# The second layer of a fused attention and MoE kernel: its first two products by Strassen's seven block products, its last product as a separate stage

## The chip, the cores and the metric

The kernel is one program on one core of a Trainium2 chip. The metric is the time on the device in microseconds (us), the median of several executions; lower is better. Engines: PE is TensorE (matmuls), PEld its weight loads, DVE VectorE, ACT ScalarE, POOL GpSimd, SP SyncE, which here issues the DMAs (SPq is its queue).

## What is computed

```python
# q, k, v: (4, 8, 576, 64), s: (4, 8, 576)
attn_out = _attn_ref(q, k, v, s)                  # causal attention, bias from a running sum of max(s, 0)
x = attn_out.transpose(0, 2, 1, 3).reshape(2304, 512)
# first layer: w_in (512, 2048), w_out (2048, 512)
h = x @ w_in;  r = maximum(h, 0);  x = (s * r * r + b) @ w_out
# second layer: w_a, w_b (512, 1536), w_out (1536, 512)
a = x @ w_a;   b = x @ w_b;        out = (a * b) @ w_out
```

The weights of both layers arrive as float64.

## The kernel before

Every matmul of the layers runs on operands that are split in a high and a low float32r part, three matmuls for one product (high by high, high by low, low by high). A matmul takes 128 rows of contraction, 128 output rows and up to 512 columns.

The order of the whole program is written by the kernel itself. Each piece of work is an op with an engine, a cost and a due time (`Plan.op`, line 65); `Plan.order` (line 111) goes through them like a list scheduler, always giving an engine the ready op with the lowest due time, and `Plan.emit` (line 206) writes the instructions in the order found. Buffers belong to a `Tag` with so many slots. A tag with `in_order` hands its slots out in the order in which the buffers were declared, whatever the due times are. An op with `room` starts only when all the buffers named there can be had at once. On the chip each engine then runs its own list strictly in that order and waits on semaphores; SP runs all DMA issues in one list.

Tokens come in nine chunks of 256 (`NCK`). Attention and the first layer take the first part of the program. `last_two` (line 884) ends the first layer for chunks 7 and 8 together: per slice f of the hidden features `h_slice` and `y_slice`. It writes y, the first layer's output, to DRAM (`y_dr`, stored transposed: 128 features by tokens) through four evictions in the two slots of `t_r`. As `last_two` goes on, the 16 slots of `t_w` (8 KB each) that hold the first layer's weights come free, one per slice.

The second layer goes over five chunks of tokens (four of 512, one of 256) and, in each, over `NF2` = 12 slices of 128 features. `y_load` (line 983) loads a chunk of y and splits it (ACT line 992, DVE line 994). `ab_unit` (line 1026) makes 12 matmuls for a and 12 for b (line 1035), copies a out of PSUM on ACT (line 1043), multiplies on DVE (line 1044) and splits the product (lines 1047, 1048). `o_unit` (line 1053) follows `LAG` = 2 units behind and adds the slice's part of the output, 3 matmuls for each tile of 128 tokens (line 1063), into four PSUM banks, which are evicted at the chunk's end (line 1072). All weights of the second layer, 18 pieces of 1 MB, stay in SBUF; `split_w` (line 425) loads a piece as float64 words, turns it to float32 with integer operations (ACT lines 441 and 444, DVE lines 448, 450, 453) and splits it (ACT line 456, DVE line 457). The two calls of `barrier` kind that matter here are `third`, at the end of attention, and `fourth` (line 958), at the end of the first layer, which reopens its SBUF and PSUM for the second.

PSUM banks: `t_h` 2, `t_y` 2, `t_s` 4 (line 298), the last replaced by `t_o` behind `fourth`.

Of the kernel before, what the change touches and what calls it, by code (L numbers as in the profile page):

```python
# [224 lines left out]
def fused_kernel(  # L225
# [732 lines left out]
    def fourth():  # L958
        moe_ctx.close()
        psat_ctx.close()  # L960
        open_pool("ph2b", ctx)
        pools["ps_o"] = ctx.enter_context(
            tc.tile_pool(name="ps_o", bufs=1, space=PSUM, side="right", reuse_waits="tile")
        )

    moe_tags = {t_x, t_xl, t_g, t_r, t_s}
    ready3 = [op("X", 0.0, 0.0, fourth, after=[o for o in plan.ops if any(b.tag in moe_tags for b in o.bufs)])]

    t_wx = tag("ph2", [P, 2, 2, DM], F32R, 3 * NF2 // 2 - NF1, "wx")
    t_wraw = tag("ph2", [P, 2, DM, 2], U32, 2, "wraw")  # L970
    t_yraw = tag("ph2", [P, 512], F32, 2, "yraw")
    t_yh = [tag("ph2", [P, 2, 512], F32R, KC, "yhl"), tag("ph2b", [P, 2, 512], F32R, KC, "yhl")]
    t_a = tag("ph2b", [P, 512], F32, 2, "a")
    t_ab = tag("ph2b", [P, 512], F32, 2, "ab")
    t_abh = tag("ph2b", [P, 2, 512], F32R, 3, "abh")
    t_ob = tag("ph2b", [P, DM], F32, 2, "ob")
    t_o = [tag("ps_o", [P, 512], F32, 1, f"o{i}") for i in range(4)]

    chunks = [(t, min(2 * N, NT - t)) for t in range(0, NT, 2 * N)]
    y_t = {}  # L980
    BASE = 500.0

    def y_load(i, pr):
        n = chunks[i][1]
        for c in range(KC):
            raw = Buf(t_yraw, f"yr{i}{c}")
            yt = Buf(t_yh[i % 2], f"yh{i}{c}")
            y_t[i, c] = yt
            af = ready3 if i % 2 else ready2
            op(SP, 0.35, pr, lambda raw=raw, c=c: nc.sync.dma_start(raw.t[:, :n], y_dr.t[i, c, :, :n]),  # L990
               r=[(y_dr, (ck, c // 2 if ck < NCK - 2 else c)) for ck in range(2 * i, min(2 * i + 2, NCK))], w=[raw], dma=262144, after=ready2)
            op(ACT, 0.55, pr, lambda raw=raw, yt=yt: nc.scalar.copy(yt.t[:, 0, :n], raw.t[:, :n]), r=[raw], w=[(yt, 0)],
               after=af)
            op(DVE, 0.65, pr, lambda raw=raw, yt=yt: nc.vector.tensor_tensor(
                out=yt.t[:, 1, :n], in0=raw.t[:, :n], in1=as32(yt.t[:, 0, :n]), op=ALU.subtract
            ), r=[raw, (yt, 0)], w=[(yt, 1)])

    ab_w, o_w = {}, {}
    n_w2 = [0]

    def w2_load(d, i, src):
        pos = BASE - 60.0 + 4.2 * n_w2[0]
        n_w2[0] += 1
        d[i] = Buf(t_wx if n_w2[0] <= 3 * NF2 // 2 - NF1 else t_w, f"w2_{n_w2[0]}")
        raw = Buf(t_wraw, f"raw2_{n_w2[0]}")
        n0 = len(plan.ops)
        split_w(raw, d[i], src, n_w2[0] % 2 == 1, pos, pos)
        plan.after(n0, ready2)
# [7 lines left out]
    plan.after = after
    for f in range(NF2):
        w2_load(ab_w, f, w2ab[f])
        if f % 2 == 0:
            w2_load(o_w, f // 2, w2o[f // 2])  # L1020
        if f == 0:
            y_load(0, BASE - 58.0)

    ab_t, o_t = {}, {}

    def ab_unit(i, f, pr):
        n = chunks[i][1]
        ps = [Buf(t_h, f"a{i}_{f}"), Buf(t_y, f"b{i}_{f}")]
        for d in range(2):
            def go(d=d):  # L1030
                w = ab_w[f].t[:, d].rearrange("p a (c f) -> p a c f", c=KC)
                m = 0
                for c in range(KC):
                    for wi, yi in ((0, 0), (0, 1), (1, 0)):
                        nc.tensor.matmul(  # L1035
                            ps[d].t[:, :n], w[:, wi, c, :], y_t[i, c].t[:, yi, :n], start=m == 0, stop=m == 3 * KC - 1
                        )
                        m += 1

            op(PE, 12 * (n / 2400 + 0.0135), M + pr, go, r=[ab_w[f], *(y_t[i, c] for c in range(KC))], w=[ps[d]], late=0.15, room=ps)  # L1040
        a, ab, hl = Buf(t_a, f"as{i}_{f}"), Buf(t_ab, f"ab{i}_{f}"), Buf(t_abh, f"abh{i}_{f}")
        e = pr - M
        op(ACT, 0.5, e, lambda: nc.scalar.copy(a.t[:, :n], ps[0].t[:, :n]), r=[ps[0]], w=[a], late=0.1, after=ready3)  # L1043
        op(DVE, 0.63, e, lambda: nc.vector.tensor_tensor(  # L1044
            out=ab.t[:, :n], in0=ps[1].t[:, :n], in1=a.t[:, :n], op=ALU.mult
        ), r=[ps[1], a], w=[ab], late=0.08)
        op(ACT, 0.55, e, lambda: nc.scalar.copy(hl.t[:, 0, :n], ab.t[:, :n]), r=[ab], w=[(hl, 0)], late=0.1)  # L1047
        op(DVE, 0.63, e, lambda: nc.vector.tensor_tensor(  # L1048
            out=hl.t[:, 1, :n], in0=ab.t[:, :n], in1=as32(hl.t[:, 0, :n]), op=ALU.subtract
        ), r=[ab, (hl, 0)], w=[(hl, 1)], late=0.08)  # L1050
        ab_t[i, f] = hl

    def o_unit(i, f, pr):
        t0, n = chunks[i]
        hl = ab_t.pop((i, f))
        for tt in range(n // P):
            if f == 0:
                o_t[i, tt] = Buf(t_o[tt], f"o{i}{tt}")
            ops_ = o_t[i, tt]

            def go(tt=tt, ops_=ops_):
                for wi, ai in ((0, 0), (1, 0), (0, 1)):
                    nc.tensor.matmul(  # L1063
                        ops_.t, hl.t[:, ai, tt * P : (tt + 1) * P], o_w[f // 2].t[:, f % 2, wi, :],
                        start=f == 0 and wi == 0 and ai == 0, stop=f == NF2 - 1 and ai == 1,
                    )
# [9 lines left out]
    todo = [(i, f) for i in range(len(chunks)) for f in range(NF2)]  # L1076
    for j, (i, f) in enumerate(todo):
        pr = BASE + 8.2 * j
        if f == 2 and i + 1 < len(chunks):
# [105 lines left out]
```

## Time and profile before

| | |
|---|---|
| median of 3 runs | 1045.38 us (1044.62, 1045.38, 1047.78) |
| span of the profiled execution, first to last instruction | 1049.0 us, 3.6 us above the median |
| PE busy | 1018.3 us, 97% of the span |
| PEld, DVE, ACT, POOL busy | 911.7, 572.3, 522.4, 34.7 us |
| mean granted clock of TensorE | 0.998 |
| DMA | 106.6 MB, 102 GB/s on average |

The page shows one execution. Its span is the only time of that execution on the page; the sum in the prediction is made against it and then set against the median. Busy time of an engine is the union of its instructions; a matmul's own duration (its mean in ns) is longer than the distance to the next one, since matmuls are pipelined, so the cost of a row of matmuls is read from the chain of work, where pieces are cut without overlap.

### The profile page before, as it was taken

What the parts mean: (1) busy time and instruction counts of PE and PEld (TensorE: products, weight loads), DVE (VectorE), ACT (ScalarE), POOL (GpSimd) and SP (SyncE); (2) the same over time, 40 slices, a digit from 0 to 9 for tenths busy, and PEclk for the clock granted to TensorE, in tenths of its full rate; (3) what the DMA queues carried; (4) which work ended last, traced back from release to release, by engine and by line L of the source; (5) the groups of instructions that cost most, each with busy time, mean ns of one, the idle gap of its engine ahead of it and who ended that gap; (6) DMA issues with size and microseconds to landing.
All of it is one profiled execution on the core that took longest, in us unless ns stands there. A gap on an engine that the chain in (4) does not pass through costs nothing.

```text
span 1049.0 us, 17029 instructions
## 1 busy us (share of the span) xinstructions
PE 1018.3 (97%) x6808; PEld 911.7 (87%) x6808; DVE 572.3 (55%) x1005; ACT 522.4 (50%) x1029; POOL 34.7 (3%) x63
## 2 busy tenths in 40 slices
PE   4698999999999999999999999999999999999998
PEld 4598999999999999999988888888888888888897
DVE  6889764578888878796688774122113111211121
ACT  4778984568787878785465652122112111111121
POOL 4121001100000000000000000000000000000000
PEclk9999999999999999999999999999999999999999
DMA  9958523456768676866634460011002000100010
GB/s 228 226 153 211 154 81 67 117 133 173 148 142 179 145 173 139 165 134 136 235 115 145 159 210 27 1 41 41 1 1 71 0 1 11 41 1 1 1 41 21
DMA packets 137103, 106.63 MB, mean 102 GB/s; under 512 B 113088, under 2 KB 120512, under 8 KB 132672
## 3 DMA queue, kind: packets, MB, share of 16 engines
q1 hardware_dynamic: 137024, 105.55, 40.3%
q8 instruction: 53, 0.87, 0.3%
q14 instruction: 26, 0.21, 0.1%
HBM read 68.46 MB, written 10.78 MB: 76 GB/s over the span
## 4 chain that ended last, share of the span: by engine, by line
PE 85%; DVE 5%; DMA 5%; ACT 3%; issue 1%; POOL 0%; SPq 0%; DVEq 0%; POOLq 0%; ACTq 0%
PE y L867 15%; PE h L847 15%; PE b L1035 14%; PE a L1035 14%; PE o L1063 14%; PE av L562 6%; PE s L612 3%; PE s L764 3%; DMA raw<-in_w2ab_dram 2%; DVE raw L450 1%; DVE w L457 1%; DMA raw<-in_w2o_dram 1%; DVE raw L453 1%; ACT raw L441 1%; DMA tr<-hl 1%
## 5 line engine op out<-in xcount | busy, mean ns | idle before, releaser
L1044 DVE TENSOR_TENSOR ab<-b,as 128x512 f32<-128x512 f32 (+1 forms) x60 | 38.2, 638 | 274.0 <-PE b L1035 274.0
L847 PE MATMUL h<-x_all,w 128*128 128x256 f32 x1344 | 180.1, 286 | 2.4 <-ACT r L816 2.4
L867 PE MATMUL y<-g,w 128*128 128x256 f32 x1344 | 181.6, 287 | 0.0
L847 PEld LDWEIGHTS h<-x_all,w 128*128 128x128 f32 x1344 | 168.8, 193 | 3.4 <-ACT r L816 2.6
L867 PEld LDWEIGHTS y<-g,w 128*128 128x128 f32 x1344 | 167.7, 192 | 1.5
L1035 PE MATMUL b<-yh,w 128*128 128x512 f32 (+1 forms) x720 | 157.6, 368 | 0.0
L1035 PE MATMUL a<-yh,w 128*128 128x512 f32 (+1 forms) x720 | 157.5, 368 | 0.0
L1063 PE MATMUL o<-w,abh 128*128 128x512 f32 x648 | 156.6, 389 | 0.0
L1035 PEld LDWEIGHTS a<-yh,w 128*128 128x128 f32 x720 | 127.0, 188 | 23.4
L1035 PEld LDWEIGHTS b<-yh,w 128*128 128x128 f32 x720 | 126.3, 189 | 22.5
L1063 PEld LDWEIGHTS o<-w,abh 128*128 128x128 f32 x648 | 120.9, 188 | 24.6
L1043 ACT COPY as<-a 128x512 f32<-128x512 f32 (+1 forms) x60 | 32.5, 544 | 178.8 <-PE a L1035 178.6
L1047 ACT CAST abh<-ab 128x512 fp32r<-128x512 f32 (+1 forms) x60 | 34.6, 579 | 129.9 <-DVE ab L1044 129.9
L562 PE MATMUL av<-tr,vt 128*64 128x320 f16 (+4 forms) x1120 | 65.0, 274 | 13.2 <-DMA tr<-hl 8.1
L562 PEld LDWEIGHTS <-vt 128*64 128x64 bf16 x1120 | 54.9, 116 | 24.0 <-issue 9.2
L526 ACT ACTIVATE hl<-p,rc 128x256 f16<-128x256 f32 (+3 forms) x128 | 66.1, 561 | 3.5 <-DVE rc L543 3.3
L528 DVE SCALAR_TENSOR_TENSOR hl<-p,rc,hl 128x256 f16<-128x256 f32 (+3 forms) x128 | 66.0, 548 | 1.3 <-ACT hl L526 1.2
L1048 DVE TENSOR_TENSOR abh<-ab,abh 128x512 fp32r<-128x512 f32 (+1 forms) x60 | 38.2, 637 | 32.4 <-ACT abh L1047 32.3
L612 PE MATMUL s<-kq 66*128 66x256 f32 (+1 forms) x128 | 44.3, 471 | 10.3 <-DMA kq<-sums 7.8
L450 DVE SCALAR_TENSOR_TENSOR raw<-raw 128x1024 uint32<-128x1024 uint32 x34 | 41.6, 1224 | 22.5 <-ACT raw L444 20.1
L441 ACT ACTIVATE raw<-raw 128x1024 f32<-128x1024 f32 x34 | 39.6, 1163 | 25.1 <-DMA raw<-in_w2ab_dram 17.4
L456 ACT CAST w<-raw 128x1024 fp32r<-128x1024 f32 x34 | 38.7, 1148 | 18.8 <-DVE raw L453 18.5
(305 smaller groups left out, 1192.1 us busy)
## 6 DMA issues: line engine op xcount, KB each, us to landing
raw<-in_w_dram SPq DMA_DIRECT2D x16, 1024.0 KB
raw<-in_w2ab_dram SPq DMA_DIRECT2D x12, 1024.0 KB
rk<-in_k_dram SPq DMA_DIRECT2D x16, 576.0 KB
raw<-in_w2o_dram SPq DMA_DIRECT2D x6, 1024.0 KB
rq<-in_q_dram SPq DMA_DIRECT2D x16, 352.0 KB
rv<-in_v_dram SPq DMA_DIRECT2D x16, 320.0 KB
out_dram<-ob SPq DMA_DIRECT2D x18, 256.0 KB
yr<-y_dr SPq DMA_DIRECT2D x16, 256.0 KB
```

The lines of the kernel that those rows point to most:

```text
L441: op(ACT, 1.07, pr, lambda: nc.scalar.activation(hi32(), hi32(), AF.Copy, scale=2.0**-112), w=[(raw, "hi")])
L450: op(DVE, 1.15, pr, lambda: nc.vector.scalar_tensor_tensor(out=lo(), in0=hi(), scalar=0x80000000, in1=lo(), op0=ALU.bitwise_and, op1=ALU.b ...
L456: op(ACT, 1.05, pr, lambda: nc.scalar.copy(wt.t[:, :, 0, :], hi32()), r=[(raw, "hi")], w=[(wt, 0)])
L526: nc.scalar.activation(o, i_, AF.Copy, scale=r_)
L528: nc.vector.scalar_tensor_tensor(out=o, in0=i_, scalar=r_, in1=place()[:, k0:k1, 0, :cols], op0=ALU.mult, op1=ALU.subtract)
L562: nc.tensor.matmul(ap.t[64 * h : 64 * h + 64, :w], vap(j, h, vi), t[:, j, a, h, :w], start=j == 0 and m == 0, stop=j == nkt - 1 and m == 4,)
L612: nc.tensor.matmul(o, qt[:66, x, h, ti * P : (ti + 1) * P], kt[:66, x, h, :w], start=True, stop=False)
L847: nc.tensor.matmul(o, w[:, wi, c, :], x_t[ck, c].t[:, xi], start=m == 0, stop=m == 3 * KC - 1)
L867: nc.tensor.matmul(o, w1_t[2 * fp + j].t[:, 1, wi, e * P : (e + 1) * P], g.t[:, gi, j], start=fp == 0 and e % 2 == 0 and j == wi == gi == ...
L1035: nc.tensor.matmul(ps[d].t[:, :n], w[:, wi, c, :], y_t[i, c].t[:, yi, :n], start=m == 0, stop=m == 3 * KC - 1)
L1044: op(DVE, 0.63, e, lambda: nc.vector.tensor_tensor(out=ab.t[:, :n], in0=ps[1].t[:, :n], in1=a.t[:, :n], op=ALU.mult), r=[ps[1], a], w=[ab] ...
L1063: nc.tensor.matmul(ops_.t, hl.t[:, ai, tt * P : (tt + 1) * P], o_w[f // 2].t[:, f % 2, wi, :], start=f == 0 and wi == 0 and ai == 0, stop= ...
```

## The change

The two products a = x w_a and b = x w_b are formed differently for the first 2048 tokens. The contraction of 512 features is cut in two halves, the 1536 output features in two halves (slice i goes with slice i + 6, so `NFH` = 6 pairs of slices) and 1024 tokens in two blocks of 512 (`NPR` = 2 such pairs). For each pair of slices i, each matrix m (a or b) and each pair of token blocks j, `group` makes seven products of 6 matmuls in place of eight, from sums and differences of blocks. The last 256 tokens are done as before (`conv`).

- The host lays `w2ab` out by blocks. `w2_slice` loads 1 MB, decodes it as before (`decode`, the first part of `split_w`), forms four block sums on POOL and splits both the blocks and the sums into two tiles of a ring of five.
- `x_pair(j)` loads the four y blocks of each feature tile, subtracts on DVE and keeps seven split operands in `t_w` for the whole stage; `x_conv` does the last 256 tokens. Their loads share `t_yraw`, 4 slots, handed out in the order of the calls: `x_pair(0)`, `x_conv`, `x_pair(1)`.
- A group uses one bank of `t_h` and two of `t_s`, taken together at its first product; products 4 to 7 add onto banks that were read in between. DVE adds bank and running sums, and for b multiplies with a, which waits in `at`.
- a*b goes to DRAM (`ab_dr`) in float32, and after all groups a last stage loads it, splits it, and multiplies with w_out (`ab_load`, `o_unit`), chunk by chunk.
- `fourth` goes; the PSUM and SBUF of the first layer stay and are reused tag by tag (`share`).

```diff
-    NF2 = w2ab.shape[0]
+    NF2 = 2 * w2ab.shape[0]
...
+    NFH = NF2 // 2
+    t_ring = tag("ph2", [P, 4, 2, 2 * P], F32R, 5, "ring")
+    t_wraw = tag("ph2", [P, 2, DM, 2], U32, 1, "wraw")
+    t_sum = tag("ph2", [P, 4, 2 * P], F32, 1, "wsum")
+    t_yraw = tag("ph2", [P, 512], F32, 4, "yraw")
+    t_su = Tag(lambda n: moe.tile([P, 2, 512], F32, tag="g", bufs=3, name=n), 3, False, t_g)
+    t_u = Tag(lambda n: moe.tile([P, 512], F32, tag="r", bufs=2, name=n), 2, False, t_r)
...
+    ab_dr = dram_buf([2, NFH, P, NT], F32, "ab_dr")
+    BASE = 610.0
+    NPR = NT // (4 * N)
...
+    def w2_slice(m, i, pos, n):
...
+        words = decode(raw, w2ab[i, m], n % 2 == 1, pos, pos)
...
+        for z, (q, x, y, f_) in enumerate((
+            (0, lambda: blk(3), lambda: blk(2), ALU.add), (1, lambda: sm.t[:, 0], lambda: blk(0), ALU.subtract),
+            (2, lambda: blk(0), lambda: blk(3), ALU.subtract), (3, lambda: blk(1), lambda: sm.t[:, 1], ALU.subtract),
+        )):
+            op(POOL, 0.75, pos + 0.1, lambda q=q, x=x, y=y, f_=f_: nc.gpsimd.tensor_tensor(out=sm.t[:, q], in0=x(), in1=y(), op=f_),
...
+        for t, k_, rd, src in ((wa, 0.0, (raw, "hi"), lambda: words(1).bitcast(F32).rearrange("p a (b n) -> p (a b) n", n=2 * P)),
+                               (ws, 0.2, sm, lambda: sm.t)):
+            op(ACT, 1.08, pos + k_, lambda t=t, src=src: nc.scalar.copy(t.t[:, :, 0], src()), r=[rd], w=[(t, 0)])
+            op(DVE, 1.12, pos + k_, lambda t=t, src=src: nc.vector.tensor_tensor(
+                out=t.t[:, :, 1], in0=src(), in1=as32(t.t[:, :, 0]), op=ALU.subtract
...
+    def x_pair(j, pos):
...
+        for kt in range(2):
...
+            split("11", r["11"])
+            sub(r["11"], r["12"], r["11"])
+            split("22", r["22"])
+            sub(r["12"], r["22"], r["12"])
+            sub(r["22"], r["22"], r["11"])
+            split("d1", r["11"])
+            split("21", r["21"])
+            sub(r["21"], r["21"], r["22"])
+            split("d2", r["22"])
+            split("d3", r["12"])
+            split("d4", r["21"])
...
+    def group(i, m, j, pr):
...
+        b1, b2, b3 = Buf(t_h, f"b1{nm}"), Buf(t_s, f"b2{nm}"), Buf(t_s, f"b3{nm}")
...
+        def product(z, bank, wt, q, n_, first, last):
+            x = X[j, n_]
+            op(PE, 1.37, M + pr + z, lambda: mm6(bank.t, wt, q, x, lambda kt, xi: x.t[:, kt, xi], first, last),
+               r=[wt, x], w=[bank], late=0.15, room=[b1, b2, b3] if z == 0 else ())
...
+        product(0.0, b1, wa, 0, "11", True, True)
...
+        op(ACT, 0.5, e, lambda: nc.scalar.copy(s1(), b1.t), r=[b1], w=[(su, 0)], late=0.1)
...
+        product(0.5, b2, ws, 1, "d2", True, True)
+        add(u2, (su, 1), s1, b2, [(su, 0)])
+        product(1.0, b3, ws, 0, "d1", True, True)
+        product(1.5, b1, wa, 1, "21", False, True)
+        if m == 0:
+            op(ACT, 0.5, e, lambda: nc.scalar.copy(at.t[:, 0], b1.t), r=[b1], w=[(at, 0)], late=0.1)
+        else:
+            times(0, lambda: b1.t, b1)
+        product(2.0, b2, ws, 2, "d3", False, True)
+        add(lambda: u3.t, u3, s1, b2, [(su, 0)])
...
+        add(dst(3, lambda: u3.t), key(3, u3), lambda: u3.t, b3, [u3])
...
+        product(2.5, b2, wa, 2, "d4", False, True)
+        add(dst(2, s1), key(2, (su, 0)), s1, b2, [(su, 0)])
...
+        product(3.0, b3, ws, 3, "22", False, True)
+        add(dst(1, u2), key(1, (su, 1)), u2, b3, [(su, 1)])
+        if m:
+            times(1, u2, (su, 1))
+            for fh in (0, 1):
+                op(SP, 0.4, e, lambda fh=fh: nc.sync.dma_start(
+                    ab_dr.t[fh, i, :, j * 4 * N : (j + 1) * 4 * N], at.t[:, 2 * fh : 2 * fh + 2].rearrange("p a n -> p (a n)")
...
+    PER = 60.0
+    for m in range(2):
+        w2_slice(m, 0, 440.0 + 10.0 * m, m)
+    x_pair(0, 500.0)
+    x_conv(BASE + 2.0)
+    x_pair(1, BASE + 1.0)
+    for i in range(NFH):
+        p0 = BASE + PER * i
+        for m in range(2):
+            group(i, m, 0, p0 + 8.0 * m)
+        for m in range(2):
+            conv(i, m, p0 + 16.0 + 4.0 * m)
+        for m in range(2):
+            group(i, m, 1, p0 + 24.0 + 8.0 * m)
+        if i + 1 < NFH:
+            for m in range(2):
+                w2_slice(m, i + 1, p0 + 4.0 + 20.0 * m, m)
...
+    for f in range(NFH):
+        o_w[f] = Buf(t_w, f"wo{f}")
...
+        split_w(raw, o_w[f], w2o[f], f % 2 == 1, EP - 50.0 + 5.0 * f, EP - 50.0 + 5.0 * f)
...
+    def o_unit(c, f, pr):
...
+            op(PE, 1.37, M + pr, go, r=[hl, o_w[f]], w=[bank], late=0.15)
...
+    for z, (c, f) in enumerate(units):
+        ab_load(c, f, EP - 20.0 + 6.0 * z)
+    for z, (c, f) in enumerate(units):
+        o_unit(c, f, EP + 6.0 * z)
```

## Rows read from the trace of the kernel before

**Rows 1.** The page: busy time of each engine, share of the span, instructions.

```profile
PE 1018.3 (97%) x6808; PEld 911.7 (87%) x6808; DVE 572.3 (55%) x1005; ACT 522.4 (50%) x1029; POOL 34.7 (3%) x63
```

**Rows 2.** The stretches: length, busy time of each engine, PEclk, DMA share, GB/s.

```profile
515.00:602.04 87.04, 86.42 (x380) 70.95 (x379) 68.70 (x76) 51.89 (x63) 0.00 (x0) 1.00 0.45 155
602.04:1044.85 442.81, 442.80 (x2088) 372.01 (x2087) 110.44 (x164) 92.36 (x157) 0.00 (x0) 1.00 0.09 29
```

**Rows 3.** The chain that ended last, in order: start, us, what.

```profile
602.04 2.72 PE a L1035 x12
604.76 2.72 PE b L1035 x12
...
618.36 2.72 PE o L1063 x12
...
1002.39 1.39 PE o L1063 x6
1003.78 1.43 PE a L1035 x12
1005.21 1.44 PE b L1035 x12
...
1040.73 4.12 PE o L1063 x18
...
1044.87 0.69 DVE ob L1072
```

**Rows 4.** Groups by line: busy us, mean ns of one, idle before and its releaser.

```profile
L450 DVE SCALAR_TENSOR_TENSOR raw<-raw 128x1024 uint32<-128x1024 uint32 x34 | 41.6, 1224 | 22.5 <-ACT raw L444 20.1 <-ACT raw L441 1.5
L457 DVE TENSOR_TENSOR w<-raw,w 128x1024 fp32r<-128x1024 f32 x34 | 41.3, 1221 | 7.0 <-ACT w L456 7.0
L448 DVE TENSOR_SCALAR raw<-raw 128x1024 uint32<-128x1024 uint32 x17 | 11.7, 687 | 1.6 <-DMA raw<-in_w2ab_dram 1.3 <-DMA raw<-in_w_dram 0.3
L1044 DVE TENSOR_TENSOR ab<-b,as 128x512 f32<-128x512 f32 (+1 forms) x60 | 38.2, 638 | 274.0 <-PE b L1035 274.0
L994 DVE TENSOR_TENSOR yh<-yr,yh 128x512 fp32r<-128x512 f32 (+1 forms) x20 | 12.1, 634 | 6.2 <-ACT yh L992 6.2
L352 POOL CAST vt<-rv 128x512 bf16<-128x512 f32 x16 | 11.3, 708 | 138.3 <-issue 84.9 <-DVE rv L354 31.4 <-PE av L562 20.3
```

**Rows 5.** Timeline where the layers meet: start, us, engine, line, what, idle before.

```profile
598.45 0.75 DVE L832 SCALAR_TENSOR_TENSOR gg<-rr,sb_b,gg 128x512 fp32r<-128x512 f32 x1
...
599.25 2.79 PE L912 MATMUL yy<-gg,w 128*128 128x512 f32 x11 [0.17 <-DVE gg L832]
...
602.02 1.79 SPq L924 DMA_DIRECT2D y_dr<-yyo  x4
...
605.05 0.68 DVE L921 COPY yyo<-yy 128x512 f32<-128x512 f32 x1
605.76 1.92 SPq L924 DMA_DIRECT2D y_dr<-yyo  x4
...
607.78 0.64 SPq L437 DMA_DIRECT2D raw<-in_w2ab_dram  x1
...
615.43 1.17 ACT L441 ACTIVATE raw<-raw 128x1024 f32<-128x1024 f32 x1 [2.04 <-DMA raw<-in_w2ab_dram]
```

**Rows 6.** Timeline inside the second layer: a unit and the operations that read it.

```profile
705.23 2.88 PE L1035 MATMUL b<-yh,w 128*128 128x512 f32 x12
...
708.22 0.69 DVE L1044 TENSOR_TENSOR ab<-b,as 128x512 f32<-128x512 f32 x1 [6.09 <-PE b L1035]
```

**Rows 7.** Slices of 4 us in the first layer, columns as in Rows 2.

```profile
88.00:92.00 4.00, 1.77 (x15) 1.56 (x14) 3.93 (x6) 2.85 (x6) 0.00 (x0) 1.00 1.35 168
92.00:96.00 4.00, 3.83 (x21) 3.65 (x22) 3.47 (x5) 4.00 (x12) 0.61 (x1) 0.69 0.48 195
96.00:100.00 4.00, 4.00 (x30) 3.87 (x29) 3.93 (x7) 3.37 (x7) 1.34 (x2) 0.88 0.01 3
```

**Rows 8.** Timeline of PE in the same place: the matmuls that ended a wait.

```profile
92.17 1.88 PE L847 MATMUL h<-x_all,w 128*128 128x256 f32 x12 [2.41 <-ACT r L816]
```

More of the change, by code (lines that the diff above doesn't have):

```diff
@@ L956, in fused_kernel @@
     ])]
[L958 to L1008, printed above, removed]
+    ready3 = [op("X", 0.0, 0.0, lambda: None, after=[o for o in plan.ops if any(b.tag is t_x for b in o.bufs)])]
@@ L1014, in after @@
                 o.wait += 1
[L1016 to L1041, printed above, removed]
-        e = pr - M
[L1043 to L1051, printed above, removed]
@@ new lines, in split2, with y_rows @@
+    def split2(rd, hi, lo, src, pr):
+        op(ACT, 0.55, pr, lambda: nc.scalar.copy(hi(), src()), r=[rd], w=[(lo[0], (lo[1], 0))])
+        op(DVE, 0.65, pr, lambda: nc.vector.tensor_tensor(out=lo[2](), in0=src(), in1=as32(hi()), op=ALU.subtract),
+           r=[rd, (lo[0], (lo[1], 0))], w=[(lo[0], (lo[1], 1))])
+    X = {}
+    NAMES = ("11", "22", "d1", "21", "d2", "d3", "d4")
+    def y_rows(u, e):
+        return [(y_dr, (ck, e // 2 if ck < NCK - 2 else e)) for ck in (2 * u, 2 * u + 1) if ck < NCK]
@@ new lines, in x_conv, with half @@
+    def x_conv(pos):
+        X["c"] = Buf(t_w, "xc")
+        n0 = len(plan.ops)
+        u = NCK // 2
+        def half(e, hl):
+            v_ = X["c"].t.rearrange("p a b n -> p (a b n)").rearrange("p (k h n) -> p k h n", k=KC, h=2)
+            return v_[:, e : e + 2, hl]
+        for e in (0, 2):
+            raw = Buf(t_yraw, f"yrc{e}")
+            src = lambda raw=raw: raw.t.rearrange("p (e n) -> p e n", e=2)
+            op(SP, 0.35, pos, lambda src=src, e=e: nc.sync.dma_start(src(), y_dr.t[u, e : e + 2, :, :N].rearrange("e p n -> p e n")),
+               r=[(y_dr, (2 * u, e + z)) for z in range(2)], w=[raw], dma=262144)
+            split2(raw, lambda e=e: half(e, 0), (X["c"], e, lambda e=e: half(e, 1)), src, pos)
+        after(n0, ready2)
@@ new lines, in fused_kernel, with conv, go @@
+    ac_t = {}
+    def conv(i, m, pr):
+        wa, _ = ring[m, i]
+        x = X["c"]
+        bank = Buf(t_y, f"bc{i}{m}")
+        e = pr - M
+        for fh in range(2):
+            def go(fh=fh):
+                o = bank.t.rearrange("p (a n) -> p a n", a=2)[:, fh]
+                xv = x.t.rearrange("p a b n -> p (a b n)").rearrange("p (k h n) -> p k h n", k=KC, h=2)
+                for kh in range(2):
+                    q = (0, 1) if fh == 0 else (3, 2)
+                    mm6(o, wa, q[kh], x, lambda kt, xi: xv[:, 2 * kh + kt, xi], kh == 0, kh == 1)
+            op(PE, 1.44, M + pr + fh, go, r=[wa, x], w=[(bank, fh)], late=0.15)
+        if m == 0:
+            ac_t[i] = Buf(t_u, f"ac{i}")
+            op(ACT, 0.5, e, lambda: nc.scalar.copy(ac_t[i].t, bank.t), r=[bank], w=[ac_t[i]], late=0.1)
+        else:
+            ac = ac_t[i]
+            op(DVE, 0.64, e, lambda: nc.vector.tensor_tensor(out=ac.t, in0=bank.t, in1=ac.t, op=ALU.mult), r=[bank], w=[ac], late=0.08)
+            op(SP, 0.4, e, lambda: nc.sync.dma_start(
+                ab_dr.t[:, i, :, NPR * 4 * N :].rearrange("h p n -> p h n"), ac.t.rearrange("p (h n) -> p h n", h=2)
+            ), r=[ac], w=[(ab_dr, (i, "c"))], dma=262144)
@@ new lines, in fused_kernel @@
+    o_w = {}
+    EP = BASE + PER * NFH
+    chunks = [(t, min(2 * N, NT - t)) for t in range(0, NT, 2 * N)]
+    hl_t = {}
+    for f in range(NFH):
+        o_w[f] = Buf(t_w, f"wo{f}")
+        if f in (1, 2):
+            hl_t[0, f - 1] = Buf(t_w, f"hl0_{f - 1}")
+        raw = Buf(t_ring if f % 2 == 0 else t_wraw, f"rawo{f}")
+        n0 = len(plan.ops)
+        split_w(raw, o_w[f], w2o[f], f % 2 == 1, EP - 50.0 + 5.0 * f, EP - 50.0 + 5.0 * f)
+        after(n0, ready2)
+    o_t = {}
+    units = [(c, f) for c in range(len(chunks)) for f in range(NFH)]
@@ new lines, in ab_load @@
+    def ab_load(c, f, pr):
+        t0, n = chunks[c]
+        if (c, f) not in hl_t:
+            hl_t[c, f] = Buf(t_w, f"hl{c}_{f}")
+        hl = hl_t[c, f]
+        j = t0 // (4 * N)
+        dep = [(ab_dr, (f, j, fh)) for fh in range(2)] if j < NPR else [(ab_dr, (f, "c"))]
+        op(SP, 0.4, pr, lambda: nc.sync.dma_start(
+            as32(hl.t[:, :, 1, :n]), ab_dr.t[:, f, :, t0 : t0 + n].rearrange("h p n -> p h n")
+        ), r=dep, w=[(hl, 1)], dma=2 * 512 * n)
+        op(ACT, 0.2 + 0.0017 * n, pr, lambda: nc.scalar.copy(hl.t[:, :, 0, :n], as32(hl.t[:, :, 1, :n])), r=[(hl, 1)], w=[(hl, 0)], late=0.1)
+        op(DVE, 0.1 + 0.002 * n, pr, lambda: nc.vector.tensor_tensor(
+            out=hl.t[:, :, 1, :n], in0=as32(hl.t[:, :, 1, :n]), in1=as32(hl.t[:, :, 0, :n]), op=ALU.subtract
+        ), r=[(hl, 0)], w=[(hl, 1)], late=0.08)
@@ L1056, in o_unit @@
+    def o_unit(c, f, pr):
+        t0, n = chunks[c]
+        hl = hl_t[c, f]
         for tt in range(n // P):
             if f == 0:
[L1058 to L1066, printed above, removed]
@@ L1068, in o_unit, with go @@
-            op(PE, 0.69, M + pr, go, r=[hl, o_w[f // 2]], w=[ops_], late=0.15)
-            if f == NF2 - 1:
-                ob = Buf(t_ob, f"ob{i}{tt}")
+                o_t[c, tt] = Buf(t_s if c % 2 == 0 else (t_h, t_y)[tt % 2], f"o{c}{tt}")
+            bank = o_t[c, tt]
+            def go(tt=tt, bank=bank):
+                for fh in range(2):
+                    for wi, ai in ((0, 0), (1, 0), (0, 1)):
+                        nc.tensor.matmul(
+                            bank.t, hl.t[:, fh, ai, tt * P : (tt + 1) * P], o_w[f].t[:, fh, wi, :],
+                            start=f == 0 and fh == wi == ai == 0, stop=f == NFH - 1 and fh == 1 and ai == 1,
+                        )
```

111 lines of the change are left out of this document (91 added, 20 removed).

## The prediction

> **What bounds the kernel now.** The page's busy times come first: PE is busy 1018.3 of 1049.0 us, all other engines far less [rows 1]. An average hides stages, so next come the stretches. In the second layer, from 602.04 us, when its first matmul starts, to 1044.85, PE is busy 442.80 of 442.81 us at full clock, while DVE works 110 us and ACT 92 [rows 2]. The stretch before it is full on PE too, but there DVE works 68.7 of 87.0 us [rows 2]. The third view is the chain of work: here it is PE alone, a piece of a, a piece of b, a piece of o, with no gap, 2.72 us for 12 matmuls of 512 columns (0.227 each) and 1.43 to 1.44 for 12 of 256 [rows 3]. So the layer is made of four chunks x 12 slices x 3 pieces x 2.72 = 391.7 us and, in the last chunk, 12 x (1.43 + 1.44 + 1.39) = 51.1 us [rows 3]; together 442.8, which is the stretch. Only fewer matmuls, or gaps between them, can move the end.
>
> **What the change takes from PE.** a and b of the first 2048 tokens cost 4 x 12 x 2 x 2.72 = 261.1 us now. In the new form there are 6 pairs of slices x 2 matrices x 2 pairs of token blocks = 24 groups of 7 products of 6 matmuls, same shape: 24 x 7 x 1.36 = 228.5 us. The saving is 32.6 us. The last 256 tokens keep 288 matmuls of 256 columns, and w_out keeps 648 of 512 columns; both only move. So PE needs 442.8 - 32.6 = 410.2 us, and the span without any gap is 1016.4.
>
> **What it adds beside PE.** One pair of slices takes PE 28 x 1.36 + 4 x 1.435 = 43.8 us. For it DVE does 14 additions and multiplications in each of two token pairs and one for the last tokens, 29 x 0.638 = 18.5 us, and for two new weight pieces 4 x 1.224 + 4 x 1.221 + 0.687 = 10.5 us [rows 4]: 29.0 us, 66% of the time PE takes. ACT does seven copies and the casts of two pieces, which is less. Neither becomes the bound by its sum. The block sums on POOL (four per piece, 256 columns wide) have no row; the nearest is a POOL cast of 512 columns at 0.708 us [rows 4]. Between that and three times that, a piece costs POOL 2.8 to 8.5 us, and a piece is due every 21.9 us while POOL has nothing else, so I take no cost; without that cover it would delay a group by the same 2.8 to 8.5. a*b to DRAM and back is 14 MB each way. The stores are read again a stage later; only the last pair of slices is stored at the end of the stage, and its first reader comes six slices into the first chunk (tokens below 1024, stored half a pair earlier) or two chunks later. Cost nothing, and its cover is the 5.44 us of PE work that each slice of the last stage has for one load. The w_out pieces (six, 4 us of DVE each) need their DVE time in the last 25 us of the group stage, where DVE is a third free, and are then needed one per 5.44 us; cost nothing. The tail is the same evictions and stores as now (from the last matmul, 1040.73 + 4.12 = 1044.85 [rows 3], to the end of the span 4.2 us).
>
> **Where PE may wait inside a group.** Product 6 adds onto the bank that DVE must have read after product 5. A round trip shows in the rows: b's last matmul ends at 708.11 and DVE starts at 708.22, 0.11 later, for 0.69 [rows 6]; PE starts 0.05 after a DVE end (598.45 + 0.75 = 599.20, then 599.25 [rows 5]). With the 0.16 by which the last matmul outlasts its place in the chain (2.88 against 2.72 [rows 3, 6]), the wait is 0.16 + 0.11 + 0.69 + 0.05 = 1.01 us if PE has nothing else. But a group takes one of two `t_h` banks and two of four `t_s` banks, so two groups are open, and the order puts the first two products of the next group (or two of `conv`) there: 2.72 us of work for 1.01 us of wait. Product 4 and product 5 have the same 2.72 us between them and what they wait for. What is left over is 1.7 us, and a weight operation of DVE that has just started takes 1.22 of it [rows 4]. So gaps should be rare. The bounds are 0 and 24 x 1.01 = 24 us; below nothing is excluded, since PE already has no idle time there to give back. I take 3 us, near the lower end, because the rows show waits of this kind hidden wherever PE has another unit, for instance when weight pieces land late (a load issued at 607.78 let ACT start at 615.43, while PE had no gap [rows 5, 2]).
>
> **Where PE may wait at the start.** The seven operands of tokens 0 to 1023 can be made before 602: they need seven slots of `t_w`, which come free one per 5.44 us from the stretch that begins at 515, and 22 DVE operations x 0.634 = 14 us [rows 4], with DVE now relieved of most of the second layer's weight pieces. The second set cannot. It needs y of chunk 7, and its loads stand behind those of `x_conv` in the slots of `t_yraw`, which need y of chunk 8. The last stores of y are issued from 605.76 to 607.68; the first batch took from 602.02 to 605.05 until the next eviction could take its buffer, 3.0 us [rows 5]. So the last y lies in DRAM at about 609.5, and by the same 3.0 us the first loads land at 612.5. From there DVE has 14 us for the second set, 1.3 for `x_conv` and some 6 for the evictions of the first two groups, 21 us, to 633.5, and about 2.5 more because the second feature tile's loads wait for four raw buffers: 636. PE has two groups (14 x 1.36 = 19.0 us) and four halves of `conv` (5.7), and is through at 602.0 + 24.8 = 626.8. From then on the products whose operands are ready first can run (11, d1 and 21, of a and of b): up to 6 x 1.36 = 8.2 us, to 635. The wait is then between 1 us (all six fit) and 9 us (none does). I take 5, the middle, as the order of the six is fixed in advance. Nothing covers it further: weights of the next pair are held back by the ring of five. Later pairs of slices have no such start; at their boundary the new block sums wait for a ring slot, some 3 us of ACT and DVE work, against 4 us until they are needed.
>
> **The sum.** 1049.0 - 32.6 + 3 + 5 = 1024.4 us of span. The runs' median lies 3.6 us below the span, so 1020.8, said as 1021. Measurement can tell changes of over 0.3%, 3 us, from none.
>
> **The rivals.**
> (1) Gaps in part: the fixed order misses the fill at about half of the groups and the start costs its 9 us. 24 x 0.5 x 1.01 = 12 us, then 1049.0 - 32.6 + 12 + 9 - 3.6 = 1034. For it: DVE is at 66% and its list is strict, so one late weight load holds back the additions behind it. Against it: the 1.7 us left over.
> (2) Slower: at product 6 nothing fills the place, and a weight operation stands ahead of the addition on DVE. Each group then waits 1.01 + 1.22 = 2.23 us, 24 times, 53.5 us: 1049.0 - 32.6 + 53.5 + 5 - 3.6 = 1071. It decides from (32.6 - 5) / 24 = 1.15 us for each group on. For it: the two open groups use every bank of `t_s`, so any late release closes the fill. Against it: a third of DVE's time is free, and banks are released 4 us before they are asked for.
> (3) The clock. After 2.41 us of waiting [rows 8], the granted clock fell to 0.69 and then 0.88 of full in two slices of 4 us, a mix of 1.2 and 2.4 GHz, though PE was busy 3.83 and 4.00 us of them [rows 7]. That is 0.31 x 4 + 0.12 x 4 = 1.7 us of lost work for one wait. If each group waited its 1.01 us and lost as much, it is 24 x 2.7 = 65 us: 1049.0 - 32.6 + 65 + 5 - 3.6 = 1083. Against it: many shorter waits in this trace left the stretches at 1.00 [rows 2]. The Trainium skill warns of just this form ("TensorE: Matmul & The Clock Gate", section "A second HAM failure mode: psum-queue depth-cycling"): a kernel that cycled through PSUM banks let PE idle in small pieces between groups of matmuls, and its clock kept falling and rising. The trace of before shows one such fall here [rows 7], and none in the second layer [rows 2].
> (4) It doesn't do what it says: the seven products cost as much as eight, since the matmuls of a product run slower than 0.227 us apart. Within 0.3% of 1045. Against it: shape, operands and number of weight loads per matmul are those of now.
>
> **How the numbers follow.** Forecast, 1012 to 1030: 0.67. Rival 1, 1030 to 1042: 0.13. Rival 2: 0.08. Rival 3: 0.04. Rival 4: 0.04. Below 1012 (gains I see no place for): 0.04. The lower end of the range is the sum without gaps, 1016.4 - 3.6 = 1012.8, said as 1012. The upper end takes in most of rival 1, 1040: 1012 to 1040 leaves out 0.04 below, 0.16 above. Faster by over 0.3%: 0.67 + 0.13 + 0.04 = 0.84. Within: 0.04. Slower: 0.12.
>
> **What would show it.** Right: PE busy without gaps in the group stage, 43.8 us for each pair of slices; the only idle time of PE near 627, released by DVE or by the y loads; the last stage's pieces 1.36 us each, no wait at its start. Wrong: PE's idle time put down to DVE additions at product 6 all through the groups, a granted clock under 1.00 behind 602, the start's wait over 9 us, or gaps each time a new pair of slices begins.

## The result, and the profile after

The changed kernel takes 1015.45 us (median of 1014.72, 1014.91, 1015.99 and 1017.40), the kernel before, on the same chip, 1045.94: ratio 0.9699, 95% interval 0.9675 to 0.9724. That is 30.5 us less; 1021 was forecast, in a range of 1012 to 1040. The profiled execution took 1017.4 us with a span of 1015.0.

The page of the changed kernel, busy times:

```profile
PE 985.3 (97%) x6664; PEld 883.5 (87%) x6664; DVE 682.1 (67%) x1127; ACT 528.7 (52%) x1003; POOL 85.2 (8%) x111
```

Against [rows 1] PE lost 33.0 us and kept its 97%; DVE gained 110 us, at almost no cost to PE. The stretches of the group stage, columns as in [rows 2]:

```profile
602.00:650.00 48.00, 47.22 (x242) 40.18 (x241) 33.33 (x50) 16.20 (x27) 3.99 (x4) 1.00 0.34 114
650.00:700.00 50.00, 49.65 (x231) 41.17 (x230) 40.11 (x52) 15.12 (x17) 10.46 (x11) 1.00 0.30 111
700.00:750.00 50.00, 50.00 (x250) 42.55 (x249) 32.59 (x44) 11.63 (x14) 9.85 (x10) 1.00 0.31 111
750.00:800.00 50.00, 50.00 (x259) 42.91 (x258) 32.36 (x43) 14.22 (x17) 8.10 (x8) 1.00 0.24 90
800.00:868.00 68.00, 68.00 (x330) 57.45 (x329) 57.26 (x71) 26.59 (x30) 3.98 (x4) 1.00 0.56 193
```

PE misses 0.78 us before 650 and 0.35 us behind it, and nothing from 700 on. The timeline of PE has both gaps, each in front of product 6 (weights `wa`, operand d4) and put down to the addition that reads product 5:

```profile
637.27 1.66 PE L1092 MATMUL b<-x1d,wa 128*128 128x512 f32 x6 [0.78 <-DVE u L1117]
...
652.38 1.52 PE L1092 MATMUL b<-x,ws 128*128 128x512 f32 x6
654.25 1.66 PE L1092 MATMUL b<-x0d,wa 128*128 128x512 f32 x6 [0.35 <-DVE u L1117]
655.74 1.52 PE L1092 MATMUL b<-x,ws 128*128 128x512 f32 x6
```

A wait costs PE about 0.3 us more than its idle time: from 652.38 to 655.74 two products take 3.36 us in place of 2.72, 0.64 more, of which 0.35 is idle. The last matmul ahead of the wait outlasts its place by 0.16, and the product behind it is longer, 1.66 for 1.52. So the two waits, 1.13 us of idle time, cost 1.7 us.

In front of the second one DVE had waited, ahead of the addition in its list, for a weight load that landed late (DVE's timeline; the addition is the last line):

```profile
650.44 0.70 DVE L457 TENSOR_SCALAR raw<-raw 128x1024 uint32<-128x1024 uint32 x1 [1.24 <-DMA raw<-in_w2ab_dram]
...
653.51 0.68 DVE L1117 TENSOR_TENSOR u<-b,su 128x512 f32<-128x512 f32 x1
```

The chain of work passes from the groups to the last stage without a break (start, us, what):

```profile
861.56 2.72 PE o L1243 x12
864.28 2.72 PE b L1092 x12
867.00 144.17 PE o L1243 x636
```

**The layer and the execution.** In this chain the second layer's first matmul starts at 599.20, against 602.04 [rows 3]. From there to the end of the span it is 415.8 us after and 1049.0 - 602.04 = 447.0 before: 31.2 us less. The other 2.8 us of the two spans lie in front of the layer. A second profile of the kernel before (below) shows that the layer's start moves by more than that from one execution of the same kernel to the next. In what follows an execution's layer is measured by the stretch from its first matmul's record (0.16 us ahead of the chain's start) to the end of the span: 447.1 us before, 416.0 after.

### The profile page after: what moved, and what is told of

Its sections match the earlier page's. It is cut to its first block, busy times and chain, and to the rows that moved or that the text cites. A ratio compares the mean times of both kernels' runs of the same rounds, so it can differ in the third digit from the quotient of the medians.

```text
span 1015.0 us, 17042 instructions
## 1 busy us (share of the span) xinstructions
PE 985.3 (97%) x6664; PEld 883.5 (87%) x6664; DVE 682.1 (67%) x1127; ACT 528.7 (52%) x1003; POOL 85.2 (8%) x111
## 4 chain that ended last, share of the span: by engine, by line
PE 92%; ACT 2%; DMA 2%; DVE 2%; POOL 1%; issue 1%; SPq 0%; POOLq 0%; DVEq 0%; ACTq 0%
PE b L1092 21%; PE y L881 16%; PE h L861 15%; PE o L1243 14%; PE av L576 6%; PE hh L914 4%; PE yy L926 4%; PE bc L1092 3%; PE s L778 3%; PE s L626 3%; DMA raw<-in_w_dram 1%; ACT hl L540 1%; DMA raw<-in_w2ab_dram 0%; ACT p L642 0%; POOL sm L1017 0%
## 5 line engine op out<-in xcount | busy, mean ns | idle before, releaser
L1243 PE MATMUL o<-wo,hl 128*128 128x512 f32 x648 | 147.2, 389 | 0.0
L1243 PEld LDWEIGHTS o<-wo,hl 128*128 128x128 f32 x648 | 121.6, 188 | 25.3
L1228 DVE TENSOR_TENSOR hl<-hl 128x1024 fp32r<-128x1024 f32 (+1 forms) x30 | 33.3, 1117 | 62.4 <-ACT hl L1227 61.8
L1092 PE MATMUL b<-x,wa 128*128 128x512 f32 x288 | 72.9, 390 | 0.0
L1227 ACT CAST hl<-hl 128x1024 fp32r<-128x1024 f32 (+1 forms) x30 | 28.7, 965 | 69.9 <-DMA hl<-ab_dr 69.9
L1092 PEld LDWEIGHTS b<-x,wa 128*128 128x128 f32 x288 | 53.7, 188 | 10.9
L1092 PE MATMUL b<-x0d,ws 128*128 128x512 f32 x216 | 54.3, 389 | 0.0
L1092 PE MATMUL b<-x1d,ws 128*128 128x512 f32 x216 | 53.9, 389 | 0.0
L1117 DVE TENSOR_TENSOR su<-b,su 128x512 f32<-128x512 f32 x48 | 33.0, 688 | 22.3 <-PE b L1092 21.2
L1092 PEld LDWEIGHTS b<-x0d,ws 128*128 128x128 f32 x216 | 40.5, 188 | 8.4
```

The source lines that it names most:

```text
L1092: nc.tensor.matmul(o, wt.t[:, q, wi, kt * P : (kt + 1) * P], hl_of(kt, xi), start=first and n == 0, stop=last and n == 5, skip_group_check ...
L1117: op(DVE, 0.64, e, lambda: nc.vector.tensor_tensor(out=dst(), in0=bank.t, in1=a(), op=ALU.add), r=[bank, *reads], w=[key], late=0.08)
L1228: op(DVE, 0.1 + 0.002 * n, pr, lambda: nc.vector.tensor_tensor(out=hl.t[:, :, 1, :n], in0=as32(hl.t[:, :, 1, :n]), in1=as32(hl.t[:, :, 0, ...
L1243: nc.tensor.matmul(bank.t, hl.t[:, fh, ai, tt * P : (tt + 1) * P], o_w[f].t[:, fh, wi, :], start=f == 0 and fh == wi == ai == 0, stop=f == ...
```

## The experiments

The first two are the kernel before and the changed kernel again, for comparison; each of the others is the changed kernel with one edit, beside the kernel before on the same chip.

### The kernel before, once more (before_again)

> The kernel before once more. Its first 600 us are the same program as in the changed kernel up to the order of a few loads. If the 2.8 us in the first layer belong to the execution, its second layer starts at another time than 602.04, by some us; if they belong to the change, at 602 again, with the stretch of the second layer 442.8 us long as before.

1047.22 us, against 1046.64 for the kernel before on the same chip: level. The stretch of its second layer:

```profile
594.97:1042.10 447.13, 442.96 (x2089) 372.27 (x2087) 111.22 (x165) 92.65 (x158) 0.00 (x0) 1.00 0.09 30
```

The layer starts 7 us sooner than in the first profile and lasts 447.13 us, as there. So the first layer's end moves by several us from one execution to the next, the second layer's length does not. That execution took 1043.86 us with a span of 1042.1: the span lies about 2 us under the execution's time, not 3.6 over it, and the first profile of before was simply a longer execution.

### The changed kernel, once more (after_again)

> The changed kernel once more, to compare the others with on the same chip: 0.970 of the kernel before, waits of PE in the second layer of about 1 us in all. The start of its second layer against that of the kernel before shows whether the 2.8 us by which the first layer ended earlier in its profile belong to the change (then 599 again) or to the execution (then another value).

Ratio 0.9707 (0.9686 to 0.9728). The layer starts at 599.71 and lasts 416.29 us, and PE's two waits are in the same two places:

```profile
637.94 1.66 PE L1092 MATMUL b<-x1d,wa 128*128 128x512 f32 x6 [0.78 <-DVE u L1117]
...
655.09 1.65 PE L1092 MATMUL b<-x0d,wa 128*128 128x512 f32 x6 [0.54 <-DVE u L1117]
```

### Eight products in place of seven (eight)

```diff
+        for q, fh, u in ((0, 0, 0), (1, 0, 1), (2, 1, 0), (3, 1, 1)):
+            bank = Buf(t_s, f"c{nm}{q}")
+            for kh in range(2):
+                x = X[j, ("11", "21")[kh] if u == 0 else ("12", "22")[kh]]
+                wq = (0, 1)[kh] if fh == 0 else (3, 2)[kh]
+                op(PE, 1.37, M + pr + 0.5 * (2 * q + kh), lambda bank=bank, x=x, wq=wq, kh=kh: mm6(
+                    bank.t, wa, wq, x, lambda kt, xi: x.t[:, kt, xi], kh == 0, kh == 1), r=[wa, x], w=[bank], late=0.15)
```

Seven products, their additions, the block sums (`ws`, `sm`) and the differences in `x_pair` go.

> The changed kernel with the same stages (a*b through DRAM, w_out last, the last 256 tokens as conv), but each group forms its four blocks directly by eight products of six matmuls; the block sums and differences are left out, the output is the same. Theory (the time goes with the number of matmuls, PE has no gap worth the name): 24 x 1.36 = 32.6 us more than the changed kernel, 1048 us, that is level with the kernel before within 3 us. Rival (part of the gain comes from the new staging, or part of the seven products' gain is eaten by gaps): clearly under 1045, or over 1051.

1045.96 us against 1047.06, ratio 0.9982 (0.9969 to 0.9995). PE waited for no one in the layer, and its stretch is

```profile
595.80:1042.50 446.70, 442.85 (x2089) 372.23 (x2087) 131.76 (x147) 104.58 (x135) 0.00 (x0) 1.00 0.33 111
```

446.7 us, 0.4 less than before. The staging, the trip through DRAM and the last stage bring next to nothing by themselves and cost nothing. From here to the changed kernel it is 446.7 - 416.0 = 30.7 us: 32.6 by the count of matmuls, less the 1.7 that the two waits cost, and 0.2 stay open. The gain is the eighth product.

### One group open at a time (one_open)

```diff
+    t_gate = Tag(lambda n: None, 1)
...
+        gate = Buf(t_gate, f"gate{nm}")
...
+               r=[wt, x], w=[bank], late=0.15, room=[gate, b1, b2, b3] if z == 0 else [gate])
...
+            op(PE, 1.37, M + pr, go, r=[hl, o_w[f]], w=[bank], late=0.15, after=last_pe if (c, f) == (0, 0) else ())
```

The last line keeps the last stage off the banks until the groups are issued.

> The changed kernel, but the next group may start only when all seven products of the last are issued. Theory (what hides the wait at product 6 is the second open group): in every pair of slices two of the four groups still find a conv behind them, the other two wait about 1.01 us, so 12 to 24 waits in all, 12 to 24 us more than the changed kernel: 1027 to 1040 us; PE's waits are put down to DVE u and are about 1 us each. Rival of the clock: each wait also costs 1.7 us at a lower granted clock: 1048 us and more, with a granted clock visibly under 1.00 in the group stage. Rival (DVE answers fast enough anyhow): under 1018 us.

1038.61 us, ratio 0.9910 (0.9886 to 0.9934). The layer lasts 439.4 us, 23.4 more than the changed kernel's. The waits of PE on the addition, us in total, times, longest:

```profile
PE b L1092 <- DVE u L1119: 15.4, 14, 3.5
```

What one looks like in PE's timeline, and the longest with the matmuls behind it:

```profile
728.67 1.67 PE L1092 MATMUL b<-x1d,wa 128*128 128x512 f32 x6 [0.79 <-DVE u L1119]
...
870.73 1.91 PE L1092 MATMUL b<-x1d,wa 128*128 128x512 f32 x6 [3.45 <-DVE u L1119]
872.46 2.93 PE L1092 MATMUL b<-x,ws 128*128 128x512 f32 x6
```

The first theory holds: without a second group the round trip at product 6 comes out, 14 times in 24 groups, ten of them with 0.78 to 0.79 us of idle time (my 1.01 holds the 0.16 by which the last matmul outlasts its place, which the profile counts as busy). The groups without a wait have a `conv` behind them. The waits make 15.4 of the 23.4 us. At about 0.3 us beyond the idle time for each, as above, they cost 4 more. The products behind the 3.45 us ran at a lower clock (the second took 2.93 for 1.52), 1.7 us by the two slices in the last section. Some 3 us are not split further.

### A copy more on DVE before the addition: one and four (late_1, late_4)

```diff
+        for _ in range(4):
+            op(DVE, 0.001, e, lambda: nc.vector.tensor_copy(u3.t, b2.t), r=[b2], w=[u3])
         add(lambda: u3.t, u3, s1, b2, [(su, 0)])
```

> The changed kernel with one more PSUM copy on DVE (0.69 us, into the tile that the addition behind it overwrites) between product 5 and the addition that product 6 waits for, in every group, its cost not told to the order. Theory (2.72 us of fill against a round trip of 1.01): 1.7 us, still hidden, at most 2 us more than the changed kernel. Rival (DVE's strict list has no slack, each delay reaches PE): 24 x 0.69 = 16 us more, 1032 us.

1020.09 us, ratio 0.9733 (0.9711 to 0.9755); the layer lasts 419.2 us, 3.2 more than the changed kernel's. The places where PE waited before get longer, and two more appear:

```profile
635.65 1.65 PE L1092 MATMUL b<-x1d,wa 128*128 128x512 f32 x6 [1.51 <-DVE u L1117]
653.50 1.66 PE L1092 MATMUL b<-x0d,wa 128*128 128x512 f32 x6 [1.22 <-DVE u L1117]
839.40 1.66 PE L1092 MATMUL b<-x0d,wa 128*128 128x512 f32 x6 [0.35 <-DVE u L1117]
867.56 32.75 PE L1245 MATMUL o<-wo,hl 128*128 128x512 f32 x143 [0.46 <-DVE su L1117]
```

In 21 of 24 groups the copy is hidden, as the theory has it; in the two that waited before (635, 653) all of it came through, and the whole is 1 us more than I allowed.

> The same with four copies, 4 x 0.61 = 2.4 us from start to start. Theory: the round trip becomes 3.4 us against 2.72 us of fill, so about 0.7 us of wait in each of 24 groups, 17 us more than the changed kernel, 1032 us; waits of PE put down to DVE u. DVE stays under its sum (66% + 22%). Rival (the fill adapts, or DVE's free third takes it): under 1018. Rival (DVE's list falls behind for good): over 1045.

1061.09 us, ratio 1.0123 (1.0098 to 1.0147): 46 us more than the changed kernel and slower than before. The number is that of the second rival, the mechanism is not: DVE does not fall behind. It has free time in the steady stretch, and each group waits once, ten of the 24 for 0.96 or 0.97 us. The steady stretch, columns as in [rows 2]:

```profile
700.00:850.00 150.00, 138.14 (x659) 112.75 (x658) 122.84 (x164) 34.86 (x42) 26.17 (x27) 1.00 0.25 90
```

The waits of PE on the addition (us in total, times, longest), and one of the usual kind in PE's timeline:

```profile
PE b L1092 <- DVE u L1117: 32.3, 24, 3.7
```
```profile
706.07 1.67 PE L1092 MATMUL b<-x1d,wa 128*128 128x512 f32 x6 [0.96 <-DVE u L1117]
```

The theory was right in kind and too small in size: the four copies, into one tile, take 2.87 us from start to end and not 2.4, so the usual wait is 0.96 and not 0.7, and the two longest are 3.7 and 3.5. That is 32.3 us. The other 14 are PE's own: it is busy 424.9 us in the layer against 411.0 in the changed kernel. About half of them is what the waits cost beyond their idle time (22 more of them than in the changed kernel, at 0.3 us); most of the rest lies behind three long waits, where the clock fell. Slices of 4 us around the second, columns as in [rows 2]:

```profile
660.00:664.00 4.00, 1.99 (x9) 1.31 (x7) 3.89 (x6) 1.06 (x1) 0.00 (x0) 1.00 0.00 0
664.00:668.00 4.00, 2.50 (x6) 2.02 (x7) 3.94 (x7) 0.00 (x0) 0.00 (x0) 0.55 0.00 0
668.00:672.00 4.00, 4.00 (x12) 3.09 (x12) 2.11 (x4) 0.00 (x0) 0.00 (x0) 0.59 0.66 262
672.00:676.00 4.00, 4.00 (x25) 3.54 (x24) 2.50 (x3) 1.71 (x2) 1.71 (x3) 1.00 0.02 4
```

### conv kept out of the start (no_fill)

```diff
+            op(PE, 1.44, M + pr + fh, go, r=[wa, x], w=[(bank, fh)], late=0.15, after=tail.get(i - 1, ()))
...
+        tail[i] = [[o for o in plan.ops if o.eng == PE][-1]]
```

In the changed kernel two pieces of the next pair's `conv` run at 627.96 and 633.50, just where I had expected PE to wait for the second set of operands. I took them for what had covered that wait:

```profile
627.96 1.60 PE L1092 MATMUL bc<-xc,wa 128*128 128x256 f32 x12
...
633.50 1.60 PE L1092 MATMUL bc<-xc,wa 128*128 128x256 f32 x12
```

> The changed kernel, but the matmuls of the last 256 tokens for a pair of slices may start only when the groups of the pair before are issued. Theory (the wait near 635, for the second set of operands, was 0.8 us and not 5 because pieces of the next pair's conv ran there, 2 x 1.43 us): PE's wait near 635 grows by about 2.9 us, to 3 to 4 us, put down to DVE u or su, and the median lies 2 to 4 us over the changed kernel. Rival (the operands were simply there sooner than I reckoned, the conv pieces only took the place of products that could have run): the wait near 635 stays under 1.5 us, and the median within 1.5 us.

Ratio 0.9715 (0.9699 to 0.9731) against 0.9707 for the changed kernel on the same chip: level. With the pieces gone the wait has the same length. It comes 35.3 us behind the layer's start (633.80 - 598.50) in place of 38.2 (637.27 - 599.04), sooner by the 2.9 us of the two pieces:

```profile
623.31 4.27 PE L1092 MATMUL b<-x,wa 128*128 128x512 f32 x18
627.42 2.88 PE L1092 MATMUL b<-x1d,ws 128*128 128x512 f32 x12
630.14 1.52 PE L1092 MATMUL b<-x,wa 128*128 128x512 f32 x6
631.50 1.52 PE L1092 MATMUL b<-x1d,ws 128*128 128x512 f32 x6
633.80 1.67 PE L1092 MATMUL b<-x1d,wa 128*128 128x512 f32 x6 [0.79 <-DVE u L1117]
```

My theory falls, and the rival's numbers hold, though not its first reason: the operands were not there much sooner than I reckoned (the last one is split at 631.6, 33.1 us behind the layer's start, against 34). PE had other work and never waited for them; 0.79 us is the bare round trip at product 6, in the one place of the group stage where the order has nothing to put there. The second open group belongs to the next pair of slices. Its products 1 and 4 need only blocks of weights and had run (two of the four `x,wa` products in the rows; a group has two). The others need block sums, and these get a slot of the ring of five only when this same product 6 has read its blocks. In the profile after it ends at 637.27 + 1.66 = 638.93, then ACT casts the sums, and PE's first product with them follows:

```profile
638.96 1.05 ACT L1021 CAST ws<-sm 128x1024 fp32r<-128x1024 f32 x1 [3.19 <-PE b L1092]
...
641.50 1.52 PE L1092 MATMUL b<-x0d,ws 128*128 128x512 f32 x6
```

### The block sums on DVE (sums_dve)

```diff
-            op(POOL, 0.75, pos + 0.1, lambda q=q, x=x, y=y, f_=f_: nc.gpsimd.tensor_tensor(out=sm.t[:, q], in0=x(), in1=y(), op=f_),
+            op(DVE, 0.4, pos + 0.1, lambda q=q, x=x, y=y, f_=f_: nc.vector.tensor_tensor(out=sm.t[:, q], in0=x(), in1=y(), op=f_),
```

> The changed kernel with the four block sums of each weight piece on DVE in place of POOL. The changed kernel's DVE splits of the blocks took 1.47 us against 1.22 for those of the sums. Theory (POOL's two-input operations run beside them and hold them up): with POOL idle both take 1.22, DVE does 12 x 4 x 0.42 = 20 us more and stays near 75% in the group stage; median within 2 us of the changed kernel. Rival (the length comes from the strided input of the blocks): they stay at 1.47. Rival for the time (DVE has no room): 5 us or more over the changed kernel, waits at product 6.

1015.64 us, ratio 0.9703 (0.9687 to 0.9719), level. Groups by line in the group stage, first of the changed kernel:

```profile
L1022 DVE TENSOR_TENSOR wa<-raw,wa 128x1024 fp32r<-128x1024 f32 x9 | 13.3, 1474 | 0.0
L1022 DVE TENSOR_TENSOR ws<-sm,ws 128x1024 fp32r<-128x1024 f32 x10 | 12.2, 1221 | 2.0 <-ACT ws L1021 2.0
L1017 POOL TENSOR_TENSOR sm<-sm,raw 128x256 f32<-128x256 f32 x9 | 11.0, 1226 | 0.7
```

and with the sums on DVE:

```profile
L1022 DVE TENSOR_TENSOR wa<-raw,wa 128x1024 fp32r<-128x1024 f32 x9 | 10.9, 1216 | 0.0
L1017 DVE TENSOR_TENSOR sm<-sm,raw 128x256 f32<-128x256 f32 x9 | 3.7, 415 | 0.0
```

With POOL idle the split of the blocks takes 1.216 us in place of 1.474, with the same strided input. So POOL had held DVE up. The sums cost DVE 0.415 each, against 0.74 to 1.85 on POOL (by line 0.75 to 1.23 on average), and PE loses nothing by it: DVE is busy 110.4 us from 700 to 850, 74%, against 105.4 in the changed kernel. The wait of 0.35 us near 654 is gone here as well. The sums are done sooner, the raw buffer comes free sooner, and the weight load that stood ahead of the addition in DVE's list was issued at 643.61 in place of 645.50, in a layer that started 1.4 us sooner. DVE's list has another order here too, so which of the two took the wait away is not shown.

## Why the prediction was right, point by point

**What bounds.** Right: PE's count of matmuls sets the end, before and after. `eight`, with the whole new staging and the old count, is level with the kernel before.

**The saving of 32.6 us.** Right within half a us. The layer went from 447.0 to 415.8 us; the sum without gaps says 447.0 - 32.6 = 414.4, the two waits bring 1.7, and the stretch behind the last matmul is 0.3 shorter (1049.0 - 1044.85 = 4.15 before, 1015.0 - 1011.17 = 3.83 after).

**Work beside PE at no cost.** Right in the sum, with two sizes off. The additions take 0.688 us each, not 0.638: the row in [rows 4] is a mean with shorter forms in it. Back to back they start 0.60 apart (614.62, 615.22, 615.82), so DVE's load came out as I said, 32.6 of 50 us in the steady stretch. POOL's sums take up to 1.85 us and lengthen a DVE split by a fifth; both stayed hidden. w_out's pieces and the loads of a*b cost PE nothing: the last stage has no wait.

**Waits inside a group: 3 us taken, 1.13 us of idle time measured, which cost 1.7.** The mechanism stands: `one_open` takes the fill away and 15.4 us of waits appear. The slack of 1.7 us stands as well: 0.7 us more on the path (`late_1`) is hidden in 21 of 24 groups, 2.9 more (`late_4`) in none. The price of a wait that nothing covers, 1.01, was near: 0.78 of idle time and 0.3. The term was too large, because only two groups of 24 wait: one met a weight load that had landed late, as I had feared for many, and one has no fill (`no_fill`).

**The start: 5 us taken, no wait for an operand measured.** This step failed in its last choice; the 0.78 us near 637, counted above, is a round trip at product 6. The estimate that the second set would be ready 34.0 us after the layer's start (636 - 602.0) was near: its last split ends at 632.0 in the profile after, 32.8 us behind 599.2. PE was through with the first groups and `conv` at 623.9, 24.7 us after the start, against 24.8. But of the bounds 1 and 9 I took the middle, on the grounds that the order of the six early products is fixed. It is fixed by a scheduler that knows when each operand is due, and it had put them in the order of readiness: `no_fill` runs seven products there in a row, with no wait for an operand. Nor was it right that nothing covers the start further. The ring of five held back only the block sums of the next pair, not its first blocks, so two of the seven products are the next pair's, and in the changed kernel two pieces of its `conv` run there as well. The lower end was the one to take. With both terms 8 us were taken and 1.7 came, which is most of the way from 1021 to 1015.

**From span to median.** I took off 3.6 us, as the difference between the profiled span and the median. It was right by size and wrong by reason: the first profile of before was a longer execution (most of it in its first 100 us, where PE is busy 74.5 us against 78.6 in `before_again`, and where the clock fell [rows 7]), and a span is about 2 us shorter than its execution's time.

**The rivals.** Rival 2 (slower, from 1.15 us for each group on) did not come, but its sum can be tested on `late_4`: waits of 1.35 us on average in 24 groups, and the kernel is slower than before by 1.2%, 14 us. That is more than the sum gives, (1.35 - 1.15) x 24 = 5 us, for it counts neither the 0.3 beyond each wait nor the clock. Rival 3 (the clock) is answered in the last section. Rivals 1 and 4 did not come.

## What to carry to other kernels

Where PE is full and the other engines have a third of their time free, fewer matmuls pay nearly in full, if every wait of the new form has another independent piece of matmul work beside it: here two open groups, 2.7 us of fill for a round trip of 1 us. Count that fill against the round trip first; it decides between minus 31 us, minus 8 (one open group) and plus 14 (2.9 us more on the path). And take an operand's lateness as a wait only after asking which other work the order would put there.

## What the runs showed of the hardware

**The clock.** In `late_4` PE waited about 1 us in every group from 700 to 850, 8% of that stretch, and the granted clock stayed at 1.00, which is 2.4 GHz. Behind waits of 2.35, 3.5 and 3.7 us (`late_4`) and of 3.45 (`one_open`) it fell, as behind the 2.41 us in the kernel before [rows 7, 8]; in the slices of `late_4` above to 0.55 and 0.59, most of both at 1.2 GHz, and a product of six matmuls took up to 2.93 us in place of 1.52. Two slices behind the 3.45 us of `one_open`, columns as in [rows 2], give 0.26 x 4 + 0.17 x 4 = 1.7 us of lost work, as rival 3 reckoned for one wait:

```profile
870.00:874.00 4.00, 3.27 (x10) 2.30 (x11) 4.00 (x6) 0.43 (x1) 0.00 (x0) 0.74 0.74 259
874.00:878.00 4.00, 4.00 (x16) 3.24 (x15) 3.09 (x4) 3.03 (x4) 0.00 (x0) 0.83 0.39 143
```

Behind waits of 1.93 and 2.07 (`late_4`) and 1.73 us (`one_open`) it did not; the product there took the usual 1.66:

```profile
845.64 1.66 PE L1092 MATMUL b<-x0d,wa 128*128 128x512 f32 x6 [1.73 <-DVE u L1119]
```

So rival 3's price holds for one long wait, and waits of about 1 us do not pay it. The Trainium skill ("TensorE: Matmul & The Clock Gate", section "A second HAM failure mode: psum-queue depth-cycling") has a kernel whose clock kept falling because it paused between groups as it cycled through PSUM banks. The runs here do not show that for pauses of about 1 us, one in each group.

**POOL beside DVE.** POOL operations with two SBUF inputs lengthened a DVE split from 1.216 to 1.474 us on average, and one beside a split lasts up to 1.85 us where the shortest take 0.74. The Trainium skill ("GPSIMD Engine Reference", section "1. Specifications") says that the two engines share SBUF interfaces, and that DVE instructions with two SBUF inputs contend there; the runs agree. I had not put a price on it.
